# Dealing heads anew to the quarters of the array in a gated linear attention kernel

## The chip, the cores and the metric

The kernel runs on one core of a Trainium2 chip. TensorE (PE) multiplies matrices into PSUM (eight banks), VectorE (DVE), ScalarE (ACT) and GpSimd (POOL) work element by element, and SyncE (SP) mostly issues DMAs. The metric is the device time of one execution in microseconds, the median over several runs. A profile shows one further execution, whose span leaves out a short stretch before the first and after the last instruction.

## The reference

A recurrence over 768 time steps, for 4 sequences and 8 heads of 48 values, is followed by a feed-forward block:

```python
for t in range(S):
    state = alpha[:, :, t, :, None] * state + np.einsum('bhd,bhe->bhde', k[:, :, t], v[:, :, t])
    y[:, :, t] = np.einsum('bhd,bhde->bhe', q[:, :, t], state)
x = np.ascontiguousarray(y.transpose(0, 2, 1, 3)).reshape(B * S, H * D)
a = x @ w1
b = x @ w2
h = a * b @ w3
return (h @ w_out).astype(np.float32)
```

The model width is 8 x 48 = 384, the inner width 1024, and there are 3072 rows.

## The kernel before, in words

**The work.** Time is cut into chunks of 128 steps: 6 a sequence, 24 in all (`N`). The first part of the program goes through the chunks, one iteration of the main loop each, and writes the attention result transposed to `xd` in DRAM. The second part is the feed-forward block, with large products split into three fp32r parts (L554). Its first half starts inside the first part: from iteration 7 on (`FIRST` is 6), products of early groups of chunks are dealt out as pieces (`run(pieces)`), up to three a chunk, so some chunks are long and some short on PE.

**One chunk.** `logs` takes the logarithm of alpha on ACT; `decays` sums it on PE and takes two exponentials (`e`, L349 and L350); `decayed` multiplies k and q by them on DVE into `qk` (L359), where each head has 64 places of which 48 are filled; `transposed` turns `qk` by PE (L381) and ACT copies the result to `qkT` (L383); `outer` makes k times v, which is added to the state T on DVE (L401, L403). Every second chunk `advance` rescales the state on POOL by three rows of decays that travel through a small DRAM tensor `ends` (L320, L331, L352, L354, L367).

**The small products.** Eight heads stand as four pairs, head 2j+i in pair j, row half i: rows 0 to 47 or 64 to 111 of the array. Outputs of 64 columns fill one half of the partitions. So there are four quarters: row half i by output half. For a chunk n, `attend_state` (L474) multiplies the state with q into two banks y (bank i for row half i), with two heads of each row half in each output half. The scores (k times q) are made for whole 128x128 blocks in the first 8 chunks (L454), and from chunk 8 on ("turned", L430) as a 128-wide and a 64-wide product per head, so that the part above the diagonal is left out; scores with i=1 are kept with their row halves swapped, and `turn_v` (L165) swaps v to match on POOL. DVE masks the scores into `ms` (L440, L457). `attend` multiplies them with v (L485; for turned chunks L482 for the upper half of time, and `attend_low`, L419, for the lower half, which is issued between the scores of the next chunk). ACT copies the two banks to a tile x (L489), and `store` later sends it to `xd` from SP (L305).

**Order.** The loop's body lists the work of several chunks: state products of n-1, scores of n, transposes of n+1, `attend` of n-1, `outer` of n, gate pieces, `decayed` of n+2. The tile framework's scheduler orders instructions on each engine by its own estimates, and `issue_after` holds some back behind marks. PSUM banks are handed out in turn from eight. SP issues the loads of k, q, alpha and v and the stores in the order written.

## Time and profile before

| | us |
|---|---|
| median of 3 runs | 462.79 (461.99 to 463.24) |
| the profiled execution's own time | 462.59 |
| its span | 460.9 |
| PE busy | 446.0 (97%) |
| DVE busy | 370.6 (80%) |
| ACT busy | 270.7 (59%) |
| POOL busy | 87.4 (19%) |

Busy times count an instruction from its start to its end; neighbours overlap, so the pitch from start to start is less than the duration. The page's slices divide the span by 40, so one slice is 11.5 us; the first part ends near 187 us, in slice 17. A timeline line gives start, length, engine, line, operation, output and inputs, shape and count, and in brackets the idle time before it and what released it.

### The profile page before, as it was taken

How to read it: one execution, taken by the hardware profiler on the slowest of the kernel's cores; microseconds unless marked ns; L12 is line 12 of the kernel's file. 1: busy time of each engine (PE TensorE's matmuls, PEld its weight loads, DVE VectorE, ACT ScalarE, POOL GpSimd, SP SyncE). 2: the span in 40 equal slices, each digit the busy share in tenths (PEclk: the TensorE clock that was granted, in tenths of full speed). 3: DMA queues.
4: the chain of work that ended last, by engine and by line, in shares of the span. 5: the costliest groups of instructions: out<-in, count | busy, mean ns of one | idle time of the engine just before them, and what ended most of it. 6: DMA issues, size and time to landing. Idle time of an engine off the chain costs nothing.

```text
span 460.9 us, 10654 instructions
## 1 busy us (share of the span) xinstructions
PE 446.0 (97%) x4080; PEld 394.6 (86%) x4080; DVE 370.6 (80%) x600; ACT 270.7 (59%) x507; POOL 87.4 (19%) x171
## 2 busy tenths in 40 slices
PE   4998999899999999999999999999999999999996
PEld 2676699898989988888888888888888999999996
DVE  2897997999979989798999899999537566776671
ACT  4685966667668563787975757566436333343430
POOL 6134332324414370012021010100000000000000
PEclk9999999999999999999999999999999999999999
DMA  9999999989999965436966364521119655665511
GB/s 174 258 215 226 263 216 208 233 208 226 188 225 186 254 153 167 138 102 187 302 193 207 118 172 133 175 70 46 48 51 288 197 151 165 188 186 158 160 53 51
DMA packets 149379, 79.95 MB, mean 173 GB/s; under 512 B 97184, under 2 KB 138784, under 8 KB 149328
## 3 DMA queue, kind: packets, MB, share of 16 engines
q1 hardware_dynamic: 143840, 64.84, 57.0%
q0 software_dynamic: 5488, 14.43, 10.5%
q8 instruction: 32, 0.52, 0.5%
q14 instruction: 19, 0.16, 0.1%
HBM read 57.19 MB, written 22.06 MB: 172 GB/s over the span
## 4 chain that ended last, share of the span: by engine, by line
PE 89%; DVE 6%; issue 2%; ACT 2%; DMA 1%; DVEq 0%; ACTq 0%
PE bank L554 73%; PE bank L381 3%; PE bank L430 3%; PE bank L482 2%; PE bank L474 2%; DVE qk L359 1%; PE bank L393 1%; PE bank L340 1%; PE bank L346 1%; DVE ms L457 1%; PE bank L454 1%; PE bank L343 1%; PE bank L419 1%; PE bank L485 1%; DMA ac<-in_alpha_dram 1%
## 5 line engine op out<-in xcount | busy, mean ns | idle before, releaser
L554 PE MATMUL bank<-x,w 128*128 128x512 f32 (+1 forms) x688 | 162.7, 374 | 1.5 <-ACT qkT L383 1.2
L554 PEld LDWEIGHTS bank<-x,w 128*128 128x128 f32 x688 | 124.8, 188 | 21.3 <-ACT qkT L383 1.5
L554 PE MATMUL bank<-w3o,ab 128*128 128x384 f32 x576 | 100.2, 336 | 0.0
L554 PEld LDWEIGHTS bank<-w3o,ab 128*128 128x128 f32 x576 | 99.9, 188 | 0.2
L554 PE MATMUL bank<-x3b,w 128*128 128x512 f32 (+1 forms) x248 | 71.9, 385 | 0.0
L579 ACT ACTIVATE bank<-bank 128x512 f32<-128x512 f32 (+1 forms) x72 | 41.0, 571 | 33.1 <-PE bank L554 33.1
L554 PEld LDWEIGHTS bank<-x3b,w 128*128 128x128 f32 x248 | 46.4, 188 | 8.3
L628 POOL DMA_DIRECT2D abd<-r x33 | 19.3, 584 | 138.1 <-DVE r L614 116.2
L678 DVE TENSOR_TENSOR ab<-abl,ab 128x1024 fp32r<-128x1024 f32 x24 | 29.4, 1224 | 14.2 <-ACT ab L677 14.2
L383 ACT COPY qkT<-bank 128x512 f32<-128x512 f32 x48 | 26.1, 599 | 23.1 <-PE bank L381 23.1
L563 ACT ACTIVATE t<-bank 128x384 f32<-128x384 f32 x24 | 11.8, 493 | 45.9 <-PE bank L554 45.9
L677 ACT ACTIVATE ab<-abl 128x1024 fp32r<-128x1024 f32 x24 | 25.5, 1062 | 21.8 <-PE bank L554 19.8
L554 PE MATMUL bank<-wo,w3T 128*128 128x384 f32 x192 | 36.3, 337 | 0.0
L554 PEld LDWEIGHTS bank<-wo,w3T 128*128 128x128 f32 x192 | 34.1, 188 | 1.2
L565 DVE SCALAR_TENSOR_TENSOR o<-bank,t 128x384 f32<-128x384 f32 x24 | 13.4, 558 | 26.1 <-issue 14.3
L249 ACT ACTIVATE power<-power,rebias 128x512 uint32<-128x512 uint32 (+1 forms) x36 | 25.2, 701 | 15.0 <-DVE power L248 14.7
L359 DVE TENSOR_TENSOR qk<-kq,e 128x768 f32<-128x768 f32 x24 | 23.2, 965 | 10.5 <-ACT e L350 7.7
L565 DVE SCALAR_TENSOR_TENSOR r<-bank,r 128x384 f32<-128x384 f32 (+1 forms) x40 | 22.9, 578 | 8.5 <-ACT r L563 5.0
L563 ACT ACTIVATE r<-bank 128x384 f32<-128x384 f32 (+1 forms) x40 | 20.8, 524 | 14.7 <-PE bank L554 12.5
L614 DVE TENSOR_TENSOR r<-bank,r 128x512 f32<-128x512 f32 x32 | 21.9, 684 | 9.2 <-PE bank L554 7.7
L679 DVE SCALAR_TENSOR_TENSOR ab<-ab,abl 128x1024 fp32r<-128x1024 f32 x24 | 29.2, 1218 | 0.0
L251 DVE SCALAR_TENSOR_TENSOR mant<-mant,raw 128x512 f32<-128x512 uint32 (+1 forms) x36 | 23.5, 652 | 2.6 <-ACT raw L244 2.6
(115 smaller groups left out, 741.7 us busy)
## 6 DMA issues: line engine op xcount, KB each, us to landing
abl<-abd SPq DMA_DIRECT2D x24, 512.0 KB, 4.2
abd<-r POOLq DMA_DIRECT2D x33, 256.0 KB, 3.5
raw<-in_moe_w_dram SPq DMA_DIRECT2D x64, 128.0 KB, 3.7
raw<-in_moe_w_dram SPq DMA_DIRECT2D x12, 512.0 KB, 5.9
kq<-in_k_dram SPq DMA_DIRECT2D x24, 192.0 KB, 5.0
kq<-in_q_dram SPq DMA_DIRECT2D x24, 192.0 KB, 5.4
xd<-x SPq DMA_DIRECT2D x48, 96.0 KB, 3.7
xT<-xd POOLq DMA_DIRECT2D x6, 768.0 KB, 5.3
```

The costliest lines, as they stand in the source:

```text
L249: nc.scalar.activation(power, power, AF.Relu, scale=2.0 ** 23, bias=rebias)
L251: nc.vector.scalar_tensor_tensor(mant, top, 2.0 ** -20, rest, op0=ALU.mult, op1=ALU.add)
L359: mark["qk", n] = nc.vector.tensor_mul(qks[n % 3][:, :, :, 0:D], st.pop(("kq", n)), st.pop(("e", n)).rearrange("p i (h d) -> p i h d", h=H ...
L383: mark["qkT", n] = nc.scalar.copy(qkT[:, :, :, ds(DP * half, DP)], tp[half]).ins
L554: nc.tensor.matmul(p, w[part][i], x[part][i], start=start and part == parts[0] and i == 0, stop=stop and part == parts[-1] and i == n - 1, ...
L563: nc.scalar.activation(t, p1, AF.Copy, scale=(1.0 + 1.0 / P) * scale)
L565: nc.vector.scalar_tensor_tensor(to, p2, scale, t, op0=ALU.mult, op1=ALU.add)
L579: nc.scalar.activation(p, p, AF.Copy, scale=1.0 + 1.0 / P)
L614: nc.vector.tensor_mul(r[0], p, r[0])
L677: nc.scalar.activation(t[:, 0], ab, AF.Copy, scale=1.0 - 2.0 ** -13)
L678: nc.vector.tensor_sub(t[:, 1], ab, t[:, 0].bitcast(FP32))
L679: nc.vector.scalar_tensor_tensor(t[:, 2], t[:, 0].bitcast(FP32), -1.0 - 1.0 / P, ab, op0=ALU.mult, op1=ALU.add)
```

## The change

Head j+4i now stands in pair j, row half i, instead of head 2j+i. `decayed` therefore makes two products per chunk, one per row half, writing every second place of `qk`; the rows in `ends` are kept in two halves (their DMAs are shaped 2x192 instead of 16x24); `outer`, `turn_v` and the v operands pick heads accordingly.

`place` deals outputs anew: the first three pairs of row half i go to output half 1-i, the last pair to output half i. In a turned chunk the state products of the previous chunk, the scores and the lower products are put into four queues, one for each quarter, and issued from whichever queue has been given the least work so far (a 128-wide product counts 2, a 64-wide one 1). Before, all state products came first, and lower products stood after each pair's scores. In chunks that are not turned, and in the last iteration, state products come pair after pair. The output banks are now taken ahead of the score banks in every chunk.

As heads of one output half no longer fill whole banks, ACT copies the outputs in four instructions (two of 128x128, two of 64x256) instead of two of 128x256, and each chunk has three stores (four heads, three heads, one head) instead of two of four heads.

```diff
-    ends = {n: dram.tile([3, DM], FP32, name=f"ends{n}") for n in range(2, N, 2) if n % NCH}
+    ends = {n: dram.tile([2, 3, DM // 2], FP32, name=f"ends{n}") for n in range(2, N, 2) if n % NCH}
...
-            mark["qk", n] = nc.vector.tensor_mul(qks[n % 3][:, :, :, 0:D], st.pop(("kq", n)),
-                                 st.pop(("e", n)).rearrange("p i (h d) -> p i h d", h=H)).ins
+            kq, e = st.pop(("kq", n)), st.pop(("e", n)).rearrange("p i (h d) -> p i h d", h=H)
+            for i in range(2):
+                heads = ds(NP * i, NP)
+                mark["qk", n] = nc.vector.tensor_mul(qks[n % 3][:, :, i::2, 0:D], kq[:, :, heads], e[:, :, heads]).ins
...
-    def attend_low(n, jj, i, half):
-
-        s, w = ds(DP * i, DP), (vts[n % 2] if i else st["v", n])
-        h = half * NP // 2 + jj
-        nc.tensor.matmul(st["y", n][0][i][ds(DP * half, DP), jj, 0:DP], w[s, h if i else 2 * h, :],
-                         st["ms", n][s, i, h, 0:DP], start=(n % NCH == 0 and jj == 0), stop=True, skip_group_check=True)
+    def place(j, i):
+
+        last_pair = j == NP - 1
+        return i if last_pair else 1 - i, (NP - 1) * i if last_pair else j + i
...
+    def attend_low(n, j, i):
+
+        s, w = ds(DP * i, DP), vts[n % 2][:, j, :] if i else st["v", n][:, j, :]
+        half, slot = place(j, i)
+        nc.tensor.matmul(st["y", n][i][ds(DP * half, DP), slot, 0:DP], w[s],
+                         st["ms", n][s, i, j, 0:DP], start=n % NCH == 0 and opens(j), stop=True, skip_group_check=True)
...
-        for j in range(NP):
-            for part in range(2):
-                for i in range(2):
-                    r, t = ds(DP * i, D), slice(DP * part, C)
-                    nc.tensor.matmul(sc[i][ds(DP * (part ^ i), DP), j, t], qkT[r, 0, j, ds(DP * part, DP)],
-                                     qkT[r, 1, j, t], start=True, stop=True)
-            if turned(n - 1):
-                for i in range(2):
-                    attend_low(n - 1, j % 2, i, i ^ (j < 2))
+        quarters = []
+        for o in range(2):
+            for i in range(2):
+                mine = [j for j in range(NP) if place(j, i)[0] == o]
+                work_of = [(2, attend_state_of, (n - 1, j, i)) for j in mine if (n - 1) % NCH]
+                work_of += [(1 + (o == i), score, (j, i, o ^ i)) for j in range(NP)]
+                work_of += [(1, attend_low, (n - 1, j, i)) for j in mine if turned(n - 1)]
+                quarters.append([0, deque(work_of)])
+        while any(x for _, x in quarters):
+            x = min((x for x in quarters if x[1]), key=lambda x: x[0])
+            cost, f, args = x[1].popleft()
+            x[0] += cost
+            f(*args)
...
+    PAIRS = [(j, i) for j in range(NP) for i in ((1, 0) if j == NP - 1 else (0, 1))]
...
     def attend_state(n):
-        qkT = st.pop(("qkT", n))
...
         if n % NCH:
-            for j, i, to in st["y", n][1]:
-                r = ds(DP * i, D)
-                nc.tensor.matmul(to, Ts[n % 2][r, j, :], qkT[r, 1, j, :],
-                                 start=(j % HP == 0), stop=False, skip_group_check=True)
+            for j, i in PAIRS:
+                attend_state_of(n, j, i)
...
-        x = work.tile([C, HP, 2, C], FP32, tag="x", name="x", bufs=4)
-        for i in range(2):
-            copied = nc.scalar.copy(x[:, :, i], y[i])
+        x = work.tile([C, NP, C], FP32, tag="x", name="x", bufs=4)
+        nc.scalar.copy(x[:, 0], y[0][:, 0])
+        nc.scalar.copy(x[DP:, 1:NP - 1], y[0][DP:, 1:NP - 1])
+        nc.scalar.copy(x[:, NP - 1], y[1][:, NP - 1])
+        copied = nc.scalar.copy(x[0:DP, 1:NP - 1], y[1][0:DP, 1:NP - 1])
...
-        to = xd.rearrange("(b h d) t -> b d h t", b=2, d=D)
-        for half in range(2):
-            later.append((to[half, :, :, ds(n * C, C)], x[ds(DP * half, D)]))
+        to = xd.rearrange("(h d) t -> d h t", d=D)[:, :, ds(n * C, C)]
+        later.append((to[:, NP - 1:2 * NP - 1], x[0:D]))
+        later.append((to[:, 0:NP - 1], x[ds(DP, D), 0:NP - 1]))
+        later.append((to[:, 2 * NP - 1:], x[ds(DP, D), NP - 1:]))
...
-        if n and not late_state:
+        if n:
+            begin_outputs(n - 1)
+        if n and not late_state and not turned(n):
             attend_state(n - 1)
```

## The prediction

> **What bounds the kernel now.** I read the page first (engine shares, slices, chain), then the stretches by window, then the timeline of each engine, and last the start of every matmul record in the trace.
>
> ```profile
> span 460.9 us, 10654 instructions
> PE 446.0 (97%) x4080; PEld 394.6 (86%) x4080; DVE 370.6 (80%) x600; ACT 270.7 (59%) x507; POOL 87.4 (19%) x171
> ...
> PE   4998999899999999999999999999999999999996
> ...
> DMA  9999999989999965436966364521119655665511
> ...
> PE 89%; DVE 6%; issue 2%; ACT 2%; DMA 1%; DVEq 0%; ACTq 0%
> ```
>
> PE ends the program, and DMA is full for the first third, which is the part the change touches. The stretches show where PE is not alone:
>
> ```profile
> 20.00:40.00 20.00, 19.73 (x294) 15.11 (x293) 16.68 (x31) 17.51 (x37) 7.75 (x12) 1.00 1.13 218
> 40.00:60.00 20.00, 17.96 (x209) 13.26 (x207) 19.31 (x32) 15.33 (x34) 6.38 (x11) 1.00 1.13 249
> 90.00:105.00 15.00, 14.99 (x255) 14.05 (x256) 14.81 (x31) 8.28 (x21) 5.03 (x11) 1.00 0.93 222
> 135.00:150.00 15.00, 15.00 (x315) 13.54 (x308) 14.28 (x27) 11.52 (x26) 5.46 (x9) 1.00 0.99 194
> ```
>
> (Columns: stretch, its us, busy PE, PEld, DVE, ACT, POOL, granted clock, DMA share, GB/s.) From about 57 us PE is dense; before that loads and DVE set the pace. One turned chunk on PE, and the two places that matter outside PE:
>
> ```profile
> 89.89 0.67 PE L474 MATMUL bank<-qkT,T 48*64 48x128 f32 x16
> 90.38 0.38 PE L430 MATMUL bank<-qkT 48*64 48x128 f32 x7
> 90.50 0.22 PE L419 MATMUL bank<-ms,v 64*64 64x64 f32 x1
> ...
> 91.60 0.71 PE L381 MATMUL bank<-ident,qk 64*128 64x64 f32 x16
> ```
> ```profile
> 34.22 0.95 DVE L359 TENSOR_TENSOR qk<-kq,e 128x768 f32<-128x768 f32 x1
> ...
> 39.95 0.96 DVE L359 TENSOR_TENSOR qk<-kq,e 128x768 f32<-128x768 f32 x1 [2.58 <-ACT raw L244]
> ...
> 46.19 0.96 DVE L359 TENSOR_TENSOR qk<-kq,e 128x768 f32<-128x768 f32 x1
> ```
> ```profile
> 49.66 0.72 ACT L249 ACTIVATE power<-power,rebias 128x512 uint32<-128x512 uint32 x1 [0.77 <-DVE power L248]
> 50.29 0.63 ACT L489 COPY x<-bank 128x256 f32<-128x256 f32 x2
> ```
>
> State products, scores and lower products take 1.71 us (89.89 to 91.60). The qk products at 34.22, 39.95 and 46.19 start 0.12 to 0.53 us behind the landing of their q load (34.02, 39.42 and 46.07 in the trace's landing records): until 46 us the loads set the pace, and the releaser named at 39.95 had ended at 39.58, as the second wait. At 50.29 PE's transposes (50.69) wait for a bank that an x copy frees.
>
> **PE in the turned chunks.** Every small fp32 matmul is two passes. The trace starts four passes, one per array quarter, within 20 ns, and the next in the same quarter 109 ns later when it is 128 columns wide (75.958, 76.067, 76.176) and 58 to 60 ns later when 64 wide (76.940, 77.000). So a 128-wide product costs its quarter 0.218 us, a 64-wide one 0.118. Before: two state products per quarter (0.436), then in the quarter of equal row and output half four wide scores and two lower products (0.872 + 0.236): 1.544; the other quarter has 1.144. After, the dealing gives the unequal quarter three state products, four narrow scores and three lower products (0.654 + 0.472 + 0.354 = 1.480) and the equal one one state, four wide scores, one lower (1.208). The interleaved order lets both run through, so the longer sets the end: -0.064 a chunk. It applies to 13 chunks (9 to 23 without 13 and 19): -0.83. Chunks 13 and 19 have no state: 1.108 to 0.990, -0.12 each. Chunk 8 has no lower products: 1.308 to 1.126, -0.18. Sum -1.25, all on dense PE. Bounds: 0 (if the mixed order runs no denser than two phases) and -1.9 (if the 0.05 us by which the first state pass, 75.798 to 75.958, is longer than the next goes too in the 13 chunks).
>
> **PE outside them.** State products that are not interleaved (chunks 2 to 6, and 24) now have three pairs in the same two quarters before the fourth pair: 0.436 to 0.654, +0.22 each; in chunk 24 lower products go from 0.236 to 0.354 as well. Chunk 24 (185.54 to 186.42 now) stands in dense PE: +0.34; bounds 0 and 0.34. The five early ones: PE waits elsewhere afterwards (the load at 34.02, the ACT copy at 50.29), so 0 of 1.1 us is taken; without that cover 1.1.
>
> **DVE.** qk becomes two products of 384 elements. One of 768 moves the next start 0.87 us on (22.12 to 22.99), one of 384 0.47 (57.31 to 57.78): +0.07 a chunk, 1.7 us in 24; by whole durations (574 ns for L602's 128x384 against 951) 0.20. In dense chunks PE covers it (DVE 14.81 of 15 by overlapping durations, some 85% by starts). Between 46.19 and 50 it is on the path: +0.07. The scheduler also pulls halves apart. Around chunk 3 the first half for chunk 5 now stands ahead of chunk 3's masks, so those wait for the load of 34.02 and move from 31.76 to some 34.7. The DVE work behind it (from 34.22: the half 0.47, masks 1.20, L262 0.60, L245 and L248 0.34 each, the other half 0.47, L403 0.27, L251 to L253 1.81) then ends at 39.7 instead of 37.3, just inside the idle time before 39.95: 0 taken, up to 2 if ACT, whose L249 waits for L248 in that run and holds x copies and exponentials, comes later still.
>
> **ACT.** Two x copies of 256 become two of 128 and two of 256 on 64 partitions. A 256 copy moves the next start 0.26 on, a 512 copy 0.47; a line through both gives 0.16 for 128 (between 0.05, nothing but the fixed part, and 0.26). Partitions don't count (L440 on DVE: 407 ns on 64, 405 on 128). So 0.84 for 0.52: +0.31 a chunk (0.10 to 0.52). Behind it on ACT stand la, the gate copies and the exponentials. PE covers it in dense chunks (ACT 8.28 to 11.52 of 15); on the path once, at 50.29, where the first bank comes 0.16 and the second 0.31 later: +0.25.
> The Trainium skill (TensorEngine Tiling (Array Packing), Performance Considerations, PSUM Bottleneck) warns that once tiling has sped up TensorE the PSUM copies can become the limit, and tells to copy across several tiles at once; the change does the opposite. The rows above say that ACT has room, so the sum has 0.25 for it; if the rule held the time would be that of the ACT rival below.
>
> **SP, POOL and DMA.** SP issues a third store per chunk, of 24 KB, with the same bytes and 512-byte rows in all. It stands ahead of the next k, q, alpha and v loads. One store issue is 0.44 us (two take 0.91 at 70.39), but SP's issues are stretched by full queues until 140, and stores land 0.25 us after the one ahead (34.88, 35.17). Ahead of the load of 46.07 there are two chunks' stores: +0.3 (0 to 0.9). Later loads run a chunk ahead. POOL's end rows go as two long descriptors instead of 16 (518 ns an issue now), the vt copies keep 64x192 (572 ns); POOL is 19% busy, so 0 on both; the bound is one issue's 0.5 us either way, should a state product come to wait for it.
>
> **Sum.** Early +0.3 +0.07 +0.25 = +0.62, turned -1.25, chunk 24 +0.34: -0.3. The profiled execution took 462.59 (span 460.9 and 1.69 around it), so it would take 462.3; the median shown, 462.79, is 0.2 above it, and 462.5 is my forecast for the median.
>
> **Rivals.** 0.3% is 1.39 us, about what a measurement of this kernel can tell from no change.
> - *The loaded start loses* (slower). Chunk 3's masks behind the load: decided at 39.95, once the displaced DVE work and the ACT run behind it pass that time. For it: only 0.2 us is spare, and ACT has 0.65 us idle a chunk there, of which the copies take 0.31. Against: the next loads reset the pace. With 2 us lost there and the rest as summed, 464.5. Chance 0.21.
> - *ACT becomes the bound* (slower). Then 0.31 in each of 24 chunks, 7.4 in all, or about half of that, 3.7, if only the short chunks without gate work feel it; for it ACT runs without a gap from 107.54 to 113.12, through a short chunk; against it the ACT shares above. 466.4. Chance 0.10.
> - *The start is free and a stall goes* (faster). At 121.30 PE waits 0.4 us for a gate bank that DVE frees behind a whole qk product; now that step stands between the halves. If the early 0.62 hides too: -1.25 + 0.34 - 0.4 = -1.3, with the first-pass gain -2.0; from the median 461.5 to 460.8, so 461.1. Chance 0.26.
> - *The interleaving brings nothing*: +0.96, 463.7. The 64-wide scores of the fourth pair start at 76.966, ahead of the two wide ones that precede them in the program (77.056), so a busy quarter does not hold the others. Chance 0.05. The Trainium skill (TensorE: Matmul & The Clock Gate, Part 3, The mechanism) has matmuls start strictly in program order, by which it would be likelier; the trace disagrees.
>
> **How the numbers follow.** The forecast has 0.38; with the fourth rival 0.43 lies within 0.3%. Faster 0.26, slower 0.31 (0.21 + 0.10). The range goes from 460.7 (the fast end of the third rival) to 465.6, inside the ACT rival, and leaves out some 2 in 10. The forecast's own is 461.4 to 464.1.
>
> **What would show it.** A turned chunk from first state product to first transpose in 1.65 us, not 1.71; chunk 24's run 0.3 longer; qk products still starting behind the q loads near 34, 40 and 46; masks of chunk 3 near 34.7; the transposes of 50.69 near 51.3; four x copies in some 0.95 us; PE stalls after 60 us no longer than now (1.36 at 84.15, 0.88 at 167.75). It is wrong if the first dense gate work (57.0) comes over 2 us later, if PE waits for ACT in short chunks, or if the mixed matmuls run in more than 1.71.

## The result and the profile after

The changed kernel took 464.74 us (463.41 to 469.99, 21 runs) beside 462.76 (461.04 to 465.20, 21 runs) for the kernel before: a ratio of 1.0061, 95% interval 1.0038 to 1.0084, slower by about 2.8 us (1.8 to 3.9). The execution profiled first was the longest of them, 469.99, and three more of the 21 were above 468; a later run of the same kernel gave a profile at 464.37, close to the median. Both are used here: the first for what its extra 5 us are, the second for the usual course.

The page of the first profile (span, busy times, slices of PE, of its granted clock and of DMA, chain of waits):

```profile
span 468.3 us, 10759 instructions
PE 449.2 (96%) x4080; PEld 397.3 (85%) x4080; DVE 372.5 (80%) x624; ACT 281.8 (60%) x555; POOL 85.8 (18%) x171
...
PE   4889899997999999999999999999999999999996
...
PEclk9999999999799999999999999999999999999999
DMA  9999999999989878337957346340118656555511
...
PE 83%; DMA 6%; DVE 3%; ACT 3%; issue 3%; POOL 1%; SPq 0%; POOLq 0%; DVEq 0%; ACTq 0%
```

In the tenth slice PE drops to 7, and in the slice behind it the granted clock does. The chain of waits had no POOL in it before; now POOL has 1% and DMA 6% instead of 1%. The page of the second profile has neither dip:

```profile
span 462.6 us, 10759 instructions
PE 446.9 (97%) x4080; PEld 395.5 (85%) x4080; DVE 372.7 (81%) x624; ACT 281.7 (61%) x555; POOL 91.5 (20%) x171
...
PE 81%; DVE 8%; issue 2%; DMA 2%; ACT 1%; SPq 0%; DVEq 0%; ACTq 0%
```

The same four stretches as before the change, in the second profile (columns: stretch, its us, busy PE, PEld, DVE, ACT, POOL, granted clock, DMA share, GB/s):

```profile
20.00:40.00 20.00, 19.33 (x276) 14.86 (x276) 18.24 (x34) 16.89 (x39) 7.89 (x12) 1.00 1.04 213
40.00:60.00 20.00, 18.49 (x235) 13.91 (x232) 17.47 (x31) 16.70 (x40) 7.25 (x11) 1.00 1.09 247
90.00:105.00 15.00, 15.00 (x258) 13.97 (x257) 14.88 (x34) 10.26 (x26) 3.59 (x8) 1.00 1.03 219
135.00:150.00 15.00, 14.33 (x289) 12.87 (x289) 13.40 (x27) 12.57 (x30) 5.84 (x9) 1.00 0.78 170
```

Between 135 and 150 us PE was busy for 15.00 of 15 us and is now busy for 14.33: there is a new wait in a stretch that had none.

**The part that came as forecast.** From the matmul records: time from the first state product (or score) of a phase to the first transpose behind it, for the phases of scores 8 to 22, in us.

```
scores of chunk    8    9   10   11   12   13   14   15   16   17   18   19   20   21   22
before           1.47 1.71 1.71 1.71 1.71 1.26 1.88 1.71 1.71 1.71 1.88 1.26 1.71 1.71 1.71
changed, 2nd     1.27 1.62 1.62 1.62 1.62 1.15 2.48 1.62 1.62 1.62 2.84 1.15 1.62 1.62 1.96
changed, 1st     1.27 1.62 1.62 1.62 1.62 1.15 5.33 1.62 1.62 1.62 2.18 1.15 1.62 1.62 1.79
```

An undisturbed phase lasts 1.62 instead of 1.71, one without state products 1.15 instead of 1.26, that of chunk 8 1.27 instead of 1.47. But the phases of chunks 14 and 18, where PE has little gate work and waits for the other engines, went from 1.88 to 2.48 and 2.84, and in the first profile one took 5.33. Over the row the second profile gains 1.23 and loses 1.81: the gain of the array is there, and more than all of it is given back in three places.

**The 5.33 us of the first profile.** POOL in before, near 105 us (start, length, engine, line, operation; in brackets the idle time before it and what ended it):

```profile
102.87 1.40 POOL L367 DMA_DIRECT2D dec<-ends  x2 [0.87 <-DMA ends<-e]
104.37 0.88 POOL L165 COPY vt<-v 64x192 f32<-64x192 f32 x2
107.45 0.58 POOL L410 TENSOR_TENSOR dec<-dec 128x4 f32<-128x4 f32 x1 [2.21 <-DMA dec<-ends]
```

and in the first profile of the changed kernel, with PE's waits there:

```profile
107.53 1.40 POOL L372 DMA_DIRECT2D dec<-ends  x2 [5.57 <-DMA ends<-e]
108.92 0.53 POOL L334 DMA_DIRECT2D ends<-ac  x1
113.49 0.20 POOL L415 TENSOR_TENSOR dec<-dec 128x4 f32<-128x4 f32 x1 [4.04 <-DMA dec<-ends]
113.77 1.34 POOL L416 TENSOR_TENSOR dec<-dec,dec 128x4 f32<-128x4 f32 x1
115.17 1.57 POOL L165 COPY vt<-v 64x192 f32<-64x192 f32 x2
```
```profile
PE bank L435 <- POOL vt L165: 2.3, 1, 2.3
PE bank L500 <- DVE ms L467: 1.0, 2, 0.5
```

Before, the copies to vt of chunk 13 stood ahead of the products for dec of chunk 14 and were done at 105.3. Now they stand behind them, so they wait for the load of dec (4.04 us), start at 115.17, and PE's lower products wait 2.26 us for them. What follows costs another 1.6 us; the stretches around it in the same profile (columns as above, the granted clock behind POOL's count):

```profile
108.00:114.00 6.00, 4.95 (x132) 4.12 (x135) 5.06 (x13) 5.07 (x12) 1.88 (x5) 1.00 0.83 139
114.00:117.00 3.00, 0.74 (x34) 0.60 (x29) 3.00 (x4) 1.77 (x5) 2.90 (x4) 0.66 1.04 203
117.00:120.00 3.00, 3.00 (x56) 2.77 (x53) 2.87 (x7) 1.20 (x3) 1.91 (x5) 0.50 1.10 283
120.00:123.00 3.00, 3.00 (x23) 2.91 (x22) 0.82 (x2) 2.05 (x6) 0.22 (x1) 0.70 0.86 170
```

After the wait PE is busy without a gap from 117 to 123 us, but at half to 0.70 of its clock; the lag behind before grows from 6.70 us at the transposes of chunk 15 to 8.27 at those of chunk 16.

**The wait in the short chunks.** State products and masks near 138 us, in before:

```profile
136.56 0.74 DVE L440 TENSOR_TENSOR ms<-bank,keep 64x256 int32<-64x256 int32 x2
...
137.73 0.67 PE L474 MATMUL bank<-qkT,T 48*64 48x128 f32 x16
```

and in the second profile of the changed kernel:

```profile
138.01 1.02 DVE L365 TENSOR_TENSOR qk<-kq,e 128x384 f32<-128x384 f32 x2
139.07 0.43 DVE L467 TENSOR_TENSOR ms<-bank,keep_turned 64x256 int32<-64x256 int32 x1
139.30 0.43 PE L500 MATMUL bank<-qkT,T 48*64 48x128 f32 x2
139.51 0.75 DVE L467 TENSOR_TENSOR ms<-bank,keep 64x256 int32<-64x256 int32 x2
...
140.40 0.44 PE L500 MATMUL bank<-qkT,T 48*64 48x128 f32 x6 [0.67 <-DVE ms L467]
```

The second output bank is one that the masks of the chunk before must free. In before DVE began the masks 1.17 us ahead of PE's state products. Now the state products come 1.6 us later than in before, the masks 2.5, and PE stops after the first product (two passes). These waits are not peculiar to the new order on PE, as runs below show.

### The profile page after: what moved, and what is told of

It is laid out like the page before. It is cut to its first block, busy times and chain, and to the rows that moved or that the text cites. A ratio compares the mean times of both kernels' runs of the same rounds, so it can differ in the third digit from the quotient of the medians.

```text
span 468.3 us, 10759 instructions
## 1 busy us (share of the span) xinstructions
PE 449.2 (96%) x4080; PEld 397.3 (85%) x4080; DVE 372.5 (80%) x624; ACT 281.8 (60%) x555; POOL 85.8 (18%) x171
## 4 chain that ended last, share of the span: by engine, by line
PE 83%; DMA 6%; DVE 3%; ACT 3%; issue 3%; POOL 1%; SPq 0%; POOLq 0%; DVEq 0%; ACTq 0%
PE bank L589 71%; DMA kq<-in_q_dram 3%; PE bank L386 2%; PE bank L445 2%; PE bank L515 2%; PE bank L500 1%; DMA dec<-ends 1%; PE bank L435 1%; PE bank L398 1%; DMA ends<-e 1%; PE bank L346 1%; PE bank L349 1%; DVE qk L365 1%; PE bank L518 1%; DMA ac<-in_alpha_dram 1%
## 5 line engine op out<-in xcount | busy, mean ns | idle before, releaser
L365 DVE TENSOR_TENSOR qk<-kq,e 128x384 f32<-128x384 f32 x48 | 26.0, 556 | 10.8 <-ACT e L353 8.7
```

The source lines that it names most:

```text
L365: mark["qk", n] = nc.vector.tensor_mul(qks[n % 3][:, :, i::2, 0:D], kq[:, :, heads], e[:, :, heads]).ins
```

## The experiments

All ratios are to the kernel before on the same chip, run side by side, with 95% intervals; 0.1% is 0.46 us.

| kernel | median us | before there | ratio |
|---|---|---|---|
| changed, first set | 464.74 | 462.76 | 1.0061 (1.0038 to 1.0084) |
| changed, again | 468.02 | 463.67 | 1.0079 (1.0052 to 1.0107) |
| before, qk split | 463.61 | 463.67 | 1.0007 (0.9977 to 1.0038) |
| changed, T behind qk | 468.07 | 463.67 | 1.0061 (1.0033 to 1.0090) |
| before's start, new from chunk 7, four stores | 469.83 | 463.67 | 1.0121 (1.0086 to 1.0157) |
| the same, vt ahead of dec | 469.25 | 464.26 | 1.0101 (1.0055 to 1.0146) |
| changed, vt ahead of dec | 466.48 | 464.26 | 1.0043 (1.0018 to 1.0069) |
| changed, three orders put back | 466.92 | 464.26 | 1.0048 (1.0023 to 1.0074) |
| before, four copies | 465.62 | 464.26 | 1.0026 (1.0003 to 1.0049) |
| before, interleaved | 464.10 | 464.29 | 0.9992 (0.9960 to 1.0024) |
| changed, not interleaved | 466.73 | 464.29 | 1.0042 (1.0009 to 1.0076) |
| before, four stores | 473.53 | 464.29 | 1.0193 (1.0147 to 1.0238) |
| changed, vt ahead, masks in order | 466.44 | 464.29 | 1.0043 (1.0014 to 1.0072) |
| before, three stores | 467.30 | 463.88 | 1.0083 (1.0048 to 1.0118) |
| changed, two stores | 465.00 | 463.88 | 1.0026 (1.0000 to 1.0053) |
| the same, states first in short chunks | 464.36 | 463.88 | 1.0013 (0.9987 to 1.0039) |
| before's start, paired stores | 464.03 | 463.88 | 1.0022 (0.9998 to 1.0046) |
| before, three stores, vt ahead of dec | 465.87 | 464.43 | 1.0029 (0.9996 to 1.0061) |
| changed, third store from ACT | 469.52 | 464.43 | 1.0109 (1.0078 to 1.0140) |

### Is it the start?

The first profile is 0.3 us late at the transposes of chunk 1 and 3.0 at those of chunk 8. Its most visible place is DVE near 32 us, where the second half of chunk 4's qk now stands behind the sum for T, which waits for POOL:

```profile
29.58 0.55 DVE L365 TENSOR_TENSOR qk<-kq,e 128x384 f32<-128x384 f32 x1
32.16 0.36 DVE L408 TENSOR_TENSOR T<-bank,T 128x192 f32<-128x192 f32 x1 [2.02 <-POOL T L417]
...
33.63 0.55 DVE L365 TENSOR_TENSOR qk<-kq,e 128x384 f32<-128x384 f32 x1
```

My first theory was this order. The first run only repeats the changed kernel.

> The changed kernel once more, for a second profile of it and for an interval beside the kernels that follow. All theories: a median near 464.7 us, some 2 us above before. The transposes of chunk 4 start about 2.9 us later than in before (34.33 against 31.42 in the first profile), those of chunk 14 about 2.4 later; the 5.9 us that the first profile lost between 108 and 118 us should not be there, since that execution lay 5 us above the median.

The median rose to 468.0, with that of before at 463.67, and the ratio stayed near its first value: 9 of 12 executions were above 466.2. The profiled one, at 464.37, had the loss of the start (2.18 at chunk 4, 1.75 at chunk 8) and no dip at 115 us, as expected.

The split of qk alone, in before:

```diff
-            mark["qk", n] = nc.vector.tensor_mul(qks[n % 3][:, :, :, 0:D], st.pop(("kq", n)),
-                                 st.pop(("e", n)).rearrange("p i (h d) -> p i h d", h=H)).ins
+            kq, e = st.pop(("kq", n)), st.pop(("e", n)).rearrange("p i (h d) -> p i h d", h=H)
+            for i in range(2):
+                heads = ds(NP * i, NP)
+                mark["qk", n] = nc.vector.tensor_mul(qks[n % 3][:, :, heads, 0:D], kq[:, :, heads], e[:, :, heads]).ins
```

> Before with one edit: the qk product of a chunk is two products of four heads each. POOL's, SP's and the matmuls' order stay as in before. Order theory (the loss of the start comes from DVE's program order, in which L252 and the sum for T now stand between the two halves): chunk 2's transposes 0.7 us later; chunk 4's second half stands behind T, but POOL's product for T is early here (28.8), so little of the 2 us wait; +0.7 to +1.2 at chunk 4, a median 0.7 to 1.2 above before. Queue theory (POOL's order, the third store): nothing, within 0.2. ACT theory (four x copies): nothing. If it takes over 2 us more, the split alone is the cause.

463.61 beside 463.67: nothing that can be told, though the DVE order around T is that of the changed kernel. The forecast of the order theory was 0.7 to 1.2; the interval reaches to 1.8.

The order of DVE put back in the changed kernel (in the main loop):

```diff
-        outer(n)
+        if 1 <= n <= 4:
+            decayed(n + 2)
+            with after_marks(("qk", n + 2)):
+                outer(n)
+        else:
+            outer(n)
```

> The changed kernel with one edit: for chunks 1 to 4 the sum for T is issued on DVE behind both halves of the qk product two chunks on, so chunk 4's second half no longer waits behind T for POOL. POOL's order stays that of the changed kernel. Order theory: qk of chunk 4 complete near 31 instead of 34.1, the transposes of chunk 4 within 1.2 us of before instead of 2.9 later, and a median some 1.7 below the changed kernel, near 463.0. Queue theory (POOL's product is late and loads and stores behind it too): the wait moves to the next consumer of T or the next load, chunk 4 or 5 is as late as now, and the median stays at 464.5. ACT theory: no change, 464.7.

Both halves now ran at 27.96, with no wait for POOL, and the time did not move (1.0061): the profile had chunk 5 3.1 us late instead of chunk 4 (chunk 4 was 1.9 late). The order theory of the start falls. That the lag of the start says little by itself was shown by a later run, whose start is before's instruction by instruction (the interleaved one, below). Its profile at chunk 6:

```profile
42.06 0.96 DVE L359 TENSOR_TENSOR qk<-kq,e 128x768 f32<-128x768 f32 x1 [3.54 <-DMA kq<-in_q_dram]
```
```profile
43.68 0.50 PE L276 MATMUL bank<-w,signs 128*128 128x512 f32 x1 [2.42 <-DVE ms L468]
```

In before the same product started at 39.95 and PE's wait was 0.85 us. The same instructions can thus be 1.9 us later at chunk 8 in one execution than in another, because a load landed later; one profile against one profile decides nothing there. The profile of before shown above is an early one: four kernels whose start is before's (this one and the three with before's start below) are 1.3 to 1.9 us behind it at the transposes of chunk 8. The ten profiles with the changed start are 1.1 to 3.0 us behind it, so whether the changed start as a whole costs something stays open.

### Is it POOL's order, or the interleaving?

Next a kernel that keeps before's heads per row, and so its start, and takes the new halves, interleaving, copies and stores (four, for its heads) from chunk 7 only:

```diff
+    def dealt(n):
+        return n >= TURNED - 1
+
+    def place(n, j, i):
+        if not dealt(n):
+            return divmod(j, NP // 2)
+        last_pair = j == NP - 1
+        return i if last_pair else 1 - i, (NP - 1) * i if last_pair else j + i
...
+        later.append((to[:, 1:2 * NP - 1:2], x[0:D, 1:]))
+        later.append((to[:, 0:2 * NP - 2:2], x[ds(DP, D), 0:NP - 1]))
+        later.append((to[:, 2 * NP - 2:2 * NP - 1], x[0:D, 0:1]))
+        later.append((to[:, 2 * NP - 1:], x[ds(DP, D), NP - 1:]))
```

> Before's dealing of heads to rows (qk whole, end rows, POOL and vt as before) throughout, and before's halves, copies and two stores up to chunk 6; from chunk 7 the three-and-one placement of the halves, the interleaving by quarter, four x copies, and four stores (its heads 1,3,5 / 0,2,4 / 6 / 7). The start is before's, instruction by instruction. If the interleaving is worth what the sum says (0.064 a chunk for 13, 0.12 for two, 0.18 for one, less 0.34 in chunk 24) and copies and stores lie beside PE: 0.9 below before, near 461.9. If ACT's copies reach the path in the dense chunks: 463.7 to 466. If the interleaving brings nothing: 462.8 to 463.1.

5.6 us above before, a miss beyond all that was expected: with the start untouched, what is done from chunk 7 on loses more than the whole change. Its undisturbed phases were 1.62 as in the changed kernel. So the loss was to be sought in POOL's order, the copies or the stores. POOL's order in the turned chunks, one edit:

```diff
-        advance(n)
+        with after_marks(*[("vt", n - 1)] * turned(n - 1)):
+            advance(n)
         turn_v(n)
```

> The changed kernel with one edit on POOL: from chunk 10 on, the products for dec of chunk n are issued behind the vt copies of chunk n - 1, as in before (the changed kernel has them ahead of those copies at chunks 12, 14 and 18). DVE, ACT and PE keep their order, instruction by instruction. Block theory (late landings of dec hold the vt copies, PE's low products wait for these over 2 us, and the clock granted afterwards is low for some microseconds): the upper half of the times goes, the median falls from 468.0 to about 464.7 and the highest stays under 467; vt near 105 us, not 115. Density theory (the interleaved matmuls themselves draw the granted clock down, whatever POOL does): median and spread stay, 467 to 468.5.

> The kernel with before's start and the new halves and interleaving from chunk 7, with the same edit on POOL. Block theory: no execution near 470 any more; median 462.5 to 464 beside some 463.7 for before, the lower end if the four copies and four stores stay beside PE. Density theory: 468 to 470 as without the edit.

In the changed kernel the ratio falls from 1.0061 and 1.0079 to 1.0043, and the highest of 12 executions is 469.1: part of the upper tail goes, not all of it, and the intervals overlap. The forecast of the block theory, a median near 464.7 and none above 467, did not come. In the other kernel it brings 0.2%. By the middle values the block of POOL is a part of the loss. With the two orders of the start put back as well, DVE's as above and POOL's by

```diff
-        nc.gpsimd.tensor_mul(dec, d[:, 0, :], d[:, 1, :])
+        with after_marks(*[("v", n + 1)] * (n == 2)):
+            nc.gpsimd.tensor_mul(dec, d[:, 0, :], d[:, 1, :])
```

> The changed kernel with three orders put back to before's: vt copies ahead of dec in the turned chunks, POOL's end row and v load of chunk 3 ahead of chunk 2's products for dec, and DVE's sum for T behind both halves of qk in chunks 1 to 4. Order theory of the start: T's product on POOL near 28.5 as in before, chunk 4's transposes within 1 us of before (2.2 to 2.9 late now), and some 1 us below the kernel with the vt edit alone, near 463.7. If the start's loss comes from the third store, the four copies and the serial state products instead: no gain over the vt edit alone, 464.7.

1.0048, no gain over the POOL edit alone: once more not these orders (its profile is still 2.7 us late at chunk 8). The order of the masks on DVE (in the interleaved phases the scheduler takes a mask of the second bank first) made no difference either:

> The changed kernel with the vt copies ahead of dec on POOL, as in the run of that edit alone, and with DVE's four mask products of a turned chunk in the order of their banks (the first bank's two, then the second's), as before has them. Mask theory: the wait of 0.4 to 0.8 us at the state products near 140 goes, some 0.5 to 1 us below the vt edit alone (2.0 above before there): 1 to 1.5 above before. If the short chunks wait for DVE's backlog and not for the order of masks: no change, 2.0 above.

It stayed at 1.0043; the profile's wait at the second state product of chunk 18's phase was 0.80 (near 142 us), and 0.84 without the edit (near 144). In `turned_scores`:

```diff
+                with after_marks(*["mask"] * ("mask" in mark)):
+                    masked = nc.vector.tensor_tensor(ms[x, i, :, t].bitcast(I32), sc[i][x, :, t].bitcast(I32),
...
+                mark["mask"] = masked.ins
```

The interleaving was then taken alone, and taken away alone. In before, with its own halves, only PE's order changed:

```diff
-        for j in range(NP):
-            for part in range(2):
-                for i in range(2):
...
+        quarters = []
+        for o in range(2):
+            for i in range(2):
+                mine = [j for j in range(NP) if j // HP == o]
...
```

> Before with one edit: in the turned chunks the state products, scores and lower products are issued interleaved by array quarter, with before's own halves. Only PE's order changes; DVE, ACT, POOL and SP keep theirs, instruction by instruction. By the sum the longest quarter stays at 1.544 us, so a phase may lose at most the seam between its two parts (0 to 0.15 a chunk): 0 to 2 us below before, 462 to 464. If the interleaved order itself makes PE wait (a score in front of a state product waits for a bank that the masks free), it is 0.5 to 1.5 above before, from the short chunks 15 and 19.

464.10 beside 464.29, and undisturbed phases of 1.70 to 1.71: interleaving without the new dealing neither gains nor costs, within the 0.4% of its interval. In the changed kernel, states first and lower products behind each pair:

```diff
-        quarters = []
...
+        if (n - 1) % NCH:
+            for j, i in PAIRS:
+                attend_state_of(n - 1, j, i)
+        for j in range(NP):
+            for part in range(2):
+                for i in range(2):
+                    score(j, i, part)
+            if turned(n - 1):
+                for i in range(2):
+                    attend_low(n - 1, j, i)
```

> The changed kernel with one edit: the state products of a chunk come first, all eight, then scores with the lower products of a pair behind each pair, as before's order has them. POOL and ACT keep the changed kernel's order. By the sum of quarters a phase takes 0.654 + 0.99 = 1.64 us instead of 1.48: 2.1 us more in 13 chunks and 0.4 in chunk 8, some 2.5 above the changed kernel, or 5 to 6 above before. If the interleaving brings nothing, it equals the changed kernel, 2.8 to 3.7 above before. If the interleaving is what costs (waits in the short chunks), it is below the changed kernel.

1.0042: not 2.5 us slower than the changed kernel, and by the middle values faster. Its undisturbed phases take 1.67 (not 1.62) and its short ones 2.03 and 2.02 (not 2.48 and 2.84). The nine undisturbed phases give 0.45 back and that of chunk 8 another 0.25; the two short ones gain 1.27 and that of chunk 22 0.29. Over all, no worth of the interleaving can be told in this program. Nor do the long short phases need it: in before with the interleaving alone they took 2.17 and 1.90, and in before with a third store, whose PE order is before's (below), 2.15 and 3.21. With one profile of each kernel, what the interleaving does to them is not shown.

### Copies and stores

The four copies, in before:

```diff
-            copied = nc.scalar.copy(x[:, :, i], y[i])
+            for half in range(2):
+                copied = nc.scalar.copy(x[ds(DP * half, DP), :, i], y[i][ds(DP * half, DP)])
```

> Before with one edit: each x copy of 256 columns is made as two copies on 64 partitions, four a chunk instead of two; the matmuls, POOL and the stores keep their order. ACT theory: about 0.5 us more of ACT a chunk, felt in the start and in the five short chunks, 1.5 to 3 us above before. If ACT's copies lie beside other work everywhere: within 0.7 of before.

1.0026, 1.2 us (0.1 to 2.3), between the two expectations. The scheduler reorders ACT and DVE with this edit in the first part too (la of 86.6 us now stands at 90.4), so this is the price of the copies together with that order. Then the stores, in before:

```diff
-            later.append((to[half, :, :, ds(n * C, C)], x[ds(DP * half, D)]))
+            for h in range(0, NP, 2):
+                later.append((to[half, :, h:h + 2, ds(n * C, C)], x[ds(DP * half, D), h:h + 2]))
```

> Before with one edit: each of the two stores of a chunk's output is made as two of two heads each, four a chunk; the matmuls keep their order. The scheduler then moves POOL's products for dec ahead of the vt copies, at more places than in the changed kernel. Queue theory (the third store and what it moves is what costs): 1 to 4 us above before, with PE waiting for vt or for a load. If stores and POOL's order cost nothing: within 0.5 of before.

9.0 us above before (6.8 to 11.0), beyond all that was expected: the largest effect of all, from the same bytes in twice as many stores. With exactly the three stores of the changed kernel:

```diff
-            later.append((to[half, :, :, ds(n * C, C)], x[ds(DP * half, D)]))
+            for h in ((0, 3), (3, 1)) if half else ((0, 4),):
+                later.append((to[half, :, ds(*h), ds(n * C, C)], x[ds(DP * half, D), ds(*h)]))
```

> Before with one edit: the store of one half is made as two, of three heads and of one, three stores a chunk as in the changed kernel; the matmuls keep their order. The scheduler then moves POOL's products for dec ahead of the vt copies at the chunks where the changed kernel has them. Store theory (the third store and the order it sets on POOL are the largest part of the loss): 2 to 4 us above before, at least half of what the changed kernel loses. If the loss comes from the start, the copies or the short chunks' interleaving: within 0.7 of before.

1.0083, 3.9 us (2.2 to 5.5): as much as the whole change loses. PE's order is before's. ACT's and DVE's are too up to 187 us, but for one swap on ACT near 116 us. Behind that both are reordered, but there nothing is lost: the profile is 2.6 us late at the transposes of chunk 23 and 2.6 at its end. What moves is POOL; near 110 us in this run:

```profile
109.89 0.19 POOL L410 TENSOR_TENSOR dec<-dec 128x4 f32<-128x4 f32 x1 [2.62 <-DMA dec<-ends]
110.16 0.20 POOL L411 TENSOR_TENSOR dec<-dec,dec 128x4 f32<-128x4 f32 x1
110.42 0.73 POOL L165 COPY vt<-v 64x192 f32<-64x192 f32 x2
```

And the other way round, the changed kernel with two stores (its output stands in another order of heads):

```diff
-        later.append((to[:, NP - 1:2 * NP - 1], x[0:D]))
-        later.append((to[:, 0:NP - 1], x[ds(DP, D), 0:NP - 1]))
-        later.append((to[:, 2 * NP - 1:], x[ds(DP, D), NP - 1:]))
+        later.append((to[:, NP:], x[0:D]))
+        later.append((to[:, 0:NP], x[ds(DP, D)]))
```

> The changed kernel with one edit: the output of a chunk goes out in two stores of four heads each, head 7 beside heads 0 to 2 and heads 3 to 6 behind them, so the rows of x stand in another order of heads than the weights and the output is another one; the work and the bytes are the same. PE, ACT and (but for one swap late) DVE keep the changed kernel's order; POOL's order goes back to before's in the turned chunks by itself. Store theory: 1.5 to 3 us below the changed kernel, 0.5 to 1.5 above before. If the stores cost nothing: 2.8 to 3.7 above before, as the changed kernel.

1.0026 instead of 1.0061 and 1.0079: 1.6 to 2.5 us by the middle values (the intervals overlap). PE's and ACT's orders are the changed kernel's to the instruction. POOL's order went back by itself, as the traces' order of its instructions between two pairs of dec loads shows (row and end are the DMAs that write rows of `ends`, from alpha and from e):

```
before               load load  vt vt  dec dec  end  vt vt  T
changed              load load  row  dec dec  vt vt  end  T  vt vt
before, 3 stores     load load  row  dec dec  vt vt  end  T  vt vt
changed, 2 stores    load load  vt vt  dec dec  end  vt vt  T
```

So it is the number of SP's stores that decides POOL's order, presumably by the scheduler's estimates of time. Putting that order back, by the edit on `advance` above, while the third store stays:

> Before with the third store, and on POOL the vt copies put ahead of the products for dec again in the turned chunks; all other engines keep the order of the run with the third store alone, which lay 3.4 us (0.83%) above before. If the store costs by the order that it sets on POOL: at most 0.3% above before. If it costs by its place in SP's queue and on the DMA engines: 0.6 to 0.9% above, as without the edit.

1.0029 instead of 1.0083: of 3.9 us about 2.5 are the order on POOL, by the middle values (the intervals overlap). How that order costs is seen in one execution only, the first profile, where PE waits 2.26 us for vt. In the run with three stores PE never waits for vt; between 60 and 187 us it waits 2.2 us for DVE's masks, in before not at all. One way to such a wait is seen there on ACT and DVE near 137 us, and it has nothing to do with vt:

```profile
136.67 0.49 ACT L564 ACTIVATE r<-bank 128x384 f32<-128x384 f32 x1 [2.46 <-DMA abd<-r]
...
138.72 0.95 DVE L359 TENSOR_TENSOR qk<-kq,e 128x768 f32<-128x768 f32 x1
139.59 0.74 DVE L440 TENSOR_TENSOR ms<-bank,keep 64x256 int32<-64x256 int32 x2
...
140.48 0.66 PE L474 MATMUL bank<-qkT,T 48*64 48x128 f32 x12 [0.62 <-DVE ms L440]
```

A gate copy on ACT waits for the landing of a gate store, which SP issues in turn with the output stores; behind it on ACT and DVE stand the exponentials, the qk product and the masks, and PE's state products wait for these. In the run with vt ahead again it is still there, 1.74 us. In before it was 1.06 us:

```profile
133.57 0.49 ACT L563 ACTIVATE r<-bank 128x384 f32<-128x384 f32 x1 [1.06 <-DMA abd<-r]
```

Moving the third store of the changed kernel from SP to ACT's queue is no cure (states first in the short chunks as in the next section):

```diff
             dst, src = later.popleft()
-            nc.sync.dma_start(out=dst, in_=src)
+            (nc.scalar if src.shape[0] == D and len(src.shape) == 3 and src.shape[1] == 1 else nc.sync).dma_start(out=dst, in_=src)
```

> The changed kernel, right output and all, with the third store issued from ACT's queue instead of SP's, and state products first in chunks 14, 18 and 22. If the third store costs by standing in SP's queue ahead of loads: 0.1 to 0.3% above before, like the kernel with two stores and the same PE order (0.13%). If it costs as a transfer: 0.4 to 0.6%. If its issue on ACT takes ACT's time in the short chunks: above 0.6%.

1.0109: ACT's own instructions now stand behind a store, and the scheduler has put ACT and DVE in another order. ACT stood idle for 1.61 us around an issue of that store near 115.7 us, by a landing of xd, and PE once waited 2.38 us for ACT (at 134.66).

### A version that beats both?

Two stores, and states first in the short chunks:

```diff
+        if n in (14, 18, 22):
+            if (n - 1) % NCH:
+                for j, i in PAIRS:
+                    attend_state_of(n - 1, j, i)
+            for j in range(NP):
+                for part in range(2):
+                    for i in range(2):
+                        score(j, i, part)
+                if turned(n - 1):
+                    for i in range(2):
+                        attend_low(n - 1, j, i)
```

> The kernel with two stores (heads of x in another order, output another one) and with one more edit on PE alone: in the chunks that start with little gate work (scores of chunks 14, 18 and 22) the state products come first and the scores behind them, as before's order has them; all others stay interleaved. Seam theory (where DVE's masks set the pace, the interleaved order puts the state products behind a score that waits for a bank): those phases go from 2.5 to 2.8 back to 2.0, some 0.8 to 1.2 below the kernel with two stores alone, within 0.5 of before or below it. If these waits are hidden later: no change.

1.0013, the best of the changed kernels, and still not below before; the short phases took 2.45 and 2.31, not 2.0. With two stores alone they had taken 2.50 and 2.29, so the gain did not come in the expected way; 1.0013 and 1.0026 can't be told apart. And the version with before's rows and start, and the four stores made once for two chunks (the edit against the kernel with before's start):

```diff
-        x = work.tile([C, NP, C], FP32, tag="x", name="x", bufs=4)
+        two, second = n < N - 1, n % 2 == 0
+        if not second or not two:
+            st["x"] = work.tile([C, NP, 2, C], FP32, tag="x2", name="x2", bufs=2)
+        x = st["x"][:, :, int(second)]
...
+        if second or not two:
+            width = (2 if two else 1) * C
```

> A version to beat both: before's rows and start; from chunk 7 the new halves, interleaved but for chunks 14, 18 and 22, masks in the order of their banks, four x copies, and one set of four stores for two chunks together, so SP issues two a chunk as before. POOL's order is before's. By the sum: 11 chunks at -0.09, two at -0.11, one at -0.2, chunk 24 at +0.3: 1.0 below before, 463.3 beside 464.3. If the four copies are on the path: equal to before or 1 above.

1.0022 instead of 1.0101 with unpaired stores: 3.7 us, from half as many stores of the same bytes and the order on POOL that goes with them, before's but for one swap (and the order of PE in three chunks and of the masks, which had brought 0.1% and nothing elsewhere). It was expected 1.0 below before. No version was measurably faster than the kernel before.

## Why the prediction was wrong

The forecast was 462.5, no measurable change, and the result is 2.8 to 3.7 us slower by the two ratios. The first median, 464.74, lies inside the range of 460.7 to 465.6, on the side and near the price (464.5) of the rival "the loaded start loses", but by luck: the costs that the runs found, in stores and copies, were put at 0.55 in the sum, and the rival's 2 us at chunk 3 are not among them.

- **The step that failed is "SP, POOL and DMA".** It gave the third store 0.3 us (0 to 0.9) for its place ahead of one load, and POOL 0 "on both", from its share of 19% and the shape of its DMAs. The third store alone, with the orders that the scheduler then sets, costs 3.9 us (2.2 to 5.5). The text counted the issue and the bytes. It did not follow the new order of POOL's instructions, in which vt stands behind a load of dec, nor the gate stores that share SP's queue and whose landing ACT waits for. "Later loads run a chunk ahead" was true of the loads and beside the point: late were a store that frees a buffer, and a copy on an engine that is idle 80% of the time. That the stores cost is shown by adding them (1.0083 and 1.0193) and by halving them in another version (from 1.0101 to 1.0022); taking the third one from the changed kernel agrees by the middle values. How much of the cost goes by vt and how much by the gate stores is argued, not shown.
- **PE in the turned chunks: right in the total, in part by luck.** Forecast -0.064, -0.12 and -0.18 a phase; measured -0.09, -0.11 and -0.20. The price of a 128-wide product in its quarter, 0.218, and the counting of quarters held for the differences. They did not hold for the phase by another order: states first was counted at 1.64 and took 1.67, interleaved at 1.48 and took 1.62. By the count, dealing without interleaving would have lost 0.10 a phase (1.64 beside 1.544); it gained 0.04 (1.67 beside 1.71). So 0.04 of the 0.09 has a cause that the count lacks.
- **"All on dense PE": wrong at two places.** The phases of chunks 14 and 18 were counted with the rest. Their 1.88 in before, beside 1.71, could have told that they are not like the others. They lost 0.60 and 0.96 in the second profile (and that of chunk 22 0.25); with the third store alone, without dealing or interleaving, 0.27 and 1.33.
- **Chunk 24: right.** From the first state product to the first gate product behind the run 1.50 us before and 1.77 now, +0.27 for a forecast of +0.34.
- **The early state products: right in size.** From the first to the last of their 16 passes 0.40 us before and 0.60 now, for a forecast of +0.22 each. Whether they cost nothing, as taken, was not measured alone.
- **DVE: the halves were pulled apart as said, and it costs nothing that can be told** (1.0007, up to 1.8 us within its interval). The masks of chunk 3 moved behind the half as forecast (34.54 us in the run of the split alone, forecast 34.7). The 2 us wait came in the first profile, at T and not at these masks, and taking it away did not move the time (1.0061).
- **ACT: too small.** Four copies were put at 0.84 us, 0.31 more than two; near 104 us they take 1.10 from start to next start (104.16 to 105.26), +0.58, just outside the bound of 0.52. The estimate had 0.16 for 128 columns and 0.26 for 256; the steps are 0.28, 0.40, 0.16 and 0.26, so only the second pair came at that. Where the step is 0.28 or 0.40 the next copy starts only behind the end of the one ahead; two of 128x256 overlapped in before (0.37 long, 0.25 from start to start):

```profile
104.16 0.27 ACT L522 COPY x<-bank 128x128 f32<-128x128 f32 x1
104.44 0.37 ACT L523 COPY x<-bank 64x256 f32<-64x256 f32 x1
...
104.84 0.27 ACT L524 COPY x<-bank 128x128 f32<-128x128 f32 x1
105.00 0.37 ACT L525 COPY x<-bank 64x256 f32<-64x256 f32 x1
```

  In time, four copies and the order that came with them cost before 1.2 us where the sum had 0.25. The Trainium skill (TensorEngine Tiling (Array Packing), Performance Considerations, PSUM Bottleneck) had warned of such copies; the runs agree in sign, and ACT is not the bound: it is 61% busy.
- **The rivals.** "ACT becomes the bound" is not what the runs show. Of "the loaded start loses" taking the wait away moved nothing that can be told, while the start as a whole stays open. "The start is free and a stall goes" failed, for new stalls came. "The interleaving brings nothing" was given 0.05; of the program's time the runs show no more than that, though the undisturbed phases did become shorter; it came by waits elsewhere and not by PE's order of starts.

What stays open: how the remaining third of a per cent divides among start, copies, short chunks and the store's place in SP's queue. Those effects are each near what these intervals can tell.

## What to carry to other kernels

One more DMA on a queue was priced here by what the scheduler did with every engine's order and by who waited for the later landings in that queue, not by its bytes or its issue: compare the order of instructions on each engine, the idle ones too, and follow each that moved behind a wait on a load to its consumer. A gain on the bound engine is to be summed only over the phases in which it does not wait; phases that are longer than their like in the profile before are the first to look at. And where one execution differs from the next by 2 us at the same place, a cause is found by adding the suspect to the old kernel and taking it from the new one, as was done with the store.

## What was not expected of the hardware

A PE wait of 2.26 us, with two of 0.5 shortly ahead of it, was followed by a granted clock of 0.66, 0.50 and 0.70 over nine microseconds; in the kernel with before's start, a wait of 1.38 us near 143 us was enough for 0.78 and 0.65 in the six microseconds behind it:

```profile
141.00:144.00 3.00, 1.62 (x22) 1.00 0.41 83
144.00:147.00 3.00, 3.00 (x84) 0.78 1.24 205
147.00:150.00 3.00, 2.92 (x38) 0.65 0.82 192
```

(PE alone: busy time, granted clock, DMA share, GB/s.) The Trainium skill (TensorE: Matmul & The Clock Gate, Part 1, What's actually happening) has the clock go to half after an idle window of about 3.4 us and come back after as long a busy one; the half clock and the length of the recovery agree with these rows, while the waits that set it off were shorter. Waits of up to 1.19 us in the dense part of before left its clock at 1.00. Nor does the length of one wait decide: in the kernel with before's start and vt ahead of dec the same wait of 1.38 us, near 141 us, left the clock at 1.00, and in the changed kernel with masks in order waits of 0.80 and 0.46 us near 142 us were followed by 0.81 and 0.62. What decides is not shown here.
